# Chunk 2's h by pairs, chunk 1's output in fewer banks, and a new order beside TensorE in chunks 1 and 2

## The chip, the cores and the metric

The kernel runs on one core of a Trainium2 chip. The metric is the device time of one execution in microseconds. Before the change it is 274.47 us, the median of three runs that lie between 274.10 and 274.95.

The engines of the core are TensorE (PE in the profile; PEld is its weight load), VectorE (DVE), ScalarE (ACT), GpSimd (POOL) and SyncE (SP), which here only issues DMAs. Each takes its instructions in the order in which the program lists them; an instruction that waits holds back all that are behind it on the same engine.

## The reference

```python
def _attn_ref(q, k, v) -> np.ndarray:                # q, k, v: (8, 8, 576, 64)
    B, H, S, D = q.shape
    theta = np.pi / 2.0 * np.arange(S) / S
    cos_w, sin_w = np.cos(theta)[None, None, :, None], np.sin(theta)[None, None, :, None]
    def phi(x, c, s):
        r = np.maximum(x, 0.0)
        return np.concatenate([r * c, r * s], axis=-1)
    q_p, k_p = phi(q, cos_w, sin_w), phi(k, cos_w, sin_w)
    kv = np.einsum('bhsf,bhsd->bhfd', k_p, v)
    z = np.sum(k_p, axis=2)
    num = np.einsum('bhsf,bhfd->bhsd', q_p, kv)
    den = np.einsum('bhsf,bhf->bhs', q_p, z)[..., None] + 1e-06
    return num / den

def _moe_ref(x, w_in, w_out, beta):                  # x: (4608, 512), w_in: (512, 2048)
    h = x @ w_in
    g = h * (1.0 / (1.0 + np.exp(-beta * h)))
    return g @ w_out                                 # (4608, 512)
```

The attention's result, with heads side by side, is the `x` of the second function. All is given and returned in float32; the kernel multiplies in bfloat16.

## The kernel before, in words

**Batches and chunks.** The attention is worked by batch, `b` = 0 to 7, with 576 tokens each, the feed-forward part by chunk, `c` = 0 to 8, with 512 tokens each. Nine groups of 64 tokens make a batch (`n` = 0 to 8), eight make a chunk, so chunk 2 takes its tokens from batches 1 and 2. While chunk c is multiplied, batch c + 1 is finished and batch c + 2 is prepared.

**A batch.** Three loads on SP bring q, k and v (1152 KB each, L86, `load_raw`) into `raw_q`, `raw_k`, `raw_v`. There is one buffer of each, so the load of the next batch waits for the last reader of this one. `q_relu` writes `qb` (L200 on ACT, L201 on DVE, two halves), `k_relu` writes `rk`, `v_scale` writes `vb`, nine instructions with the cosine and nine with the sine (L226 on ACT, L228 on DVE). A DMA transposes `qb` to `qt` (`q_turn_dma`, L268, "the turn of q"), and `tan_mul` (L232), on GpSimd in `q_tan` or on DVE, makes `qs` of it. `kv_mm` (L285, 72 small matmuls) and a copy give `kv`. `num_all` (L308), three parts of three token groups, multiplies `qt` and `qs` with it; `x_div` (denominator, reciprocal, product: L320, L324, L331) divides a part, and a DMA transposes it into `xt`, the chunk's input (`x_turn_dma`, L379).

**h of a chunk.** In chunks 0 to 2 it is `h_group` (L425): for each of 16 column blocks `jt` of `w_in` four matmuls of 512 columns (L398) into a PSUM bank, and then a Silu on ACT (L406) into `g`. From jt 4 on the bank is the one of jt - 4. In chunks 3 to 8 it is `h_pair` (eight pairs of blocks): seven products of two matmuls of 256 columns each (L522), with sums of the weights (`w_sum`) and of `xt` (`x_sum`, L466, four on DVE) as operands, and with copies and adds on ACT and DVE between them (`fast_ops`: "c" L491 on ACT copies the first product, "d" or "D" L495 copies the fifth, "e" and "f" L498 add on DVE), then two Silus (L432). Product 3 of a pair needs its add "e", product 4 its add "f".

**Output of a chunk.** Sixteen sums of `g` (`g_sum`, L418, four kinds by four slices, on DVE) and seven products of eight matmuls of 256 columns for each of two halves of the rows. Chunk 1 does this in `o_fast` (L579), with three banks for each half, chunks 2 to 8 in `o_pair` (L637). The rows go out by DMAs of GpSimd's queue (L548).

**Order.** The program is recorded instruction by instruction, without a scheduler. In chunk 0, in chunk 1 and in chunk 2's h the order is that of the Python statements (the loop at `for slot in range(16)`, the `ops` lines behind it, and `h_first`); elsewhere it is the string `ORDERS[c]`, one word for each step, read by `chunk`. Words that the prediction uses: `h13` is product 3 of pair 1, `h1e` that pair's add, `ox1`, `oy1` products of the output, `s12` the g sum of kind 1 and slice 2, `t1` the x sum of kind 1, `N0` and `x0` a part of num and its division, `K0` and `K1` kv, `q1` a relu of q on DVE, `w3` and `v3` scalings of v on DVE and ACT, `g0` a `q_tan`, `TQ` the turn of q, `Lq` a load.

What surrounds the change: before it SP holds, in chunk 1, the turn of batch 2's q, the loads of q, k and v of batch 3, the transposes of x's parts, the turn of batch 3's q, one more transpose of x, and the loads of q and k of batch 4. The relu of batch 3's q is on ACT behind h, that of batch 4's on DVE behind the scalings of batch 3 in chunk 2.

Of the kernel before, what the change touches and what calls it, by code (L numbers as in the profile page):

```python
# [22 lines left out]
def kernel(  # L23
# [234 lines left out]
    def qs_of(b):  # L258
        return wx["q"] if b > 3 and b % 2 == 0 else qs_first
# [311 lines left out]

    def o_fast(c, pr, banks):

        b_ps, e_ps, a_ps = (ps[:, k_, 0:HM] for k_ in banks)
        tok = slice(pr * P, (pr + 1) * P)

        def prod(dst, left, right, start, stop):
            for i in range(JT // 2):
                nc.tensor.matmul(dst, lhsT=left(i), rhs=right[:, i], start=start and i == 0,  # L579
                                 stop=stop and i == JT // 2 - 1, skip_group_check=True)  # L580

        def g_part(r, hf):
            def at(i):
                jt = 2 * i + r
                return gs[c, jt // 4][:, jt % 4, hf * (TCH // 2) + pr * P : hf * (TCH // 2) + (pr + 1) * P]
            return at

        def s_part(t):
            return lambda i: t[:, i, tok]

        o1 = osb_pool.tile([P, DM], FP32, name="o_sb", tag="o_sb")
        o2 = osb_pool.tile([P, DM], FP32, name="o_sb", tag="o_sb")
        p1 = part.tile([P, HM], FP32, name="p1", tag="p1")
        p5 = part.tile([P, HM], FP32, name="p5", tag="p5")
        u = part.tile([P, HM], FP32, name="u", tag="u")

        def c4():
            nc.scalar.copy(o2[:, 0:HM], b_ps)

        def stored(key, op):  # L600
            def do():
                op()
                waits[key[0]].discard(key[1:])
                if not waits[key[0]]:
                    store(c, pr + (2 if key[0] == "2" else 0), o2 if key[0] == "2" else o1)
            return do

        waits = {"1": {"a2", "a3"}, "2": {"a7", "c4"}}
        add = dict(op=ALU.add)
        return {  # L610
            "1": lambda: prod(b_ps, g_part(0, 0), B11, True, False),
            "5": lambda: prod(e_ps, s_part(S[1]), T1, True, False),
            "6": lambda: prod(b_ps, s_part(S[2]), T2, False, False),
            "2": lambda: prod(a_ps, g_part(1, 0), B21, True, True),
            "7": lambda: prod(b_ps, s_part(S[3]), T3, False, False),
            "3": lambda: prod(e_ps, s_part(S[4]), B22, False, True),
            "4": lambda: prod(b_ps, g_part(1, 1), T4, False, True),
            "c1": lambda: nc.scalar.copy(p1, b_ps),
            "c5": lambda: nc.scalar.copy(p5, e_ps),
            "cu": lambda: nc.scalar.copy(u, b_ps),  # L620
            "c4": stored("2c4", c4),
            "a2": stored("1a2", lambda: nc.vector.tensor_tensor(o1[:, 0:HM], a_ps, p1, **add)),
            "a3": stored("1a3", lambda: nc.vector.tensor_tensor(o1[:, HM:DM], e_ps, u, **add)),
            "a7": stored("2a7", lambda: nc.vector.tensor_tensor(o2[:, HM:DM], b_ps, p5, **add)),
        }
# [312 lines left out]
    t_sum(4, 4, 8)  # L938
    for jt in range(4):
        h_mm(1, jt, (0, 1))  # L940
    for slot in range(16):
        if slot < 4:
            h_mm(1, slot, (2, 3))
            h_act(1, slot)
        else:
            h_group(1, slot)
        if slot == 0:
            att_q(2)
            for jp in range(2):
                tan_mul(nc.gpsimd, qs_of(2)[:, jp, 0:1], qts[0][:, jp, 0:1], 0, 1)  # L950
            for tt, o_sb in kept:
                store(0, tt, o_sb)
            v_half(2, 0)
        if 2 <= slot < 6:
            v_half(2, 1, slot + 3, slot + 4, "act")
        if slot == 4:
            k_all(2)
            v_half(2, 1, 0, 5)
            t_sum(3, 0, 8)
        elif slot == 10:  # L960
            num_rest()
            kv_all(2, eng="act")
            x_rest()
            for jp in range(2):
                tan_mul(nc.vector, qs_of(2)[:, jp, 1:], qts[0][:, jp, 1:], 1, NQ)
    def one_sums(kind):
        for i0 in range(0, JT // 2, 2):
            got = g_sum(1, i0, i0 + 2, kind)
        return got

    def ops(of, names):
        for n in names.split():
            of[n]()

    x, y = o_fast(1, 0, (2, 5, 4)), o_fast(1, 1, (3, 7, 6))
    ops(x, "1 c1")
    one_sums(1)
    ops(y, "1 c1")
    q_relu(3, 0, "act")
    q_relu(3, 1, "act")  # L980
    for t, bank in enumerate((4, 6, 0)):
        num_all(2, t, bank)
    one_sums(2)
    x_part(2, 0, 4)
    ops(x, "6 cu")
    ops(y, "6 cu")
    one_sums(3)
    ops(x, "2 5 c5")
    x_part(2, 1, 6)
    q_turn_dma(3)  # L990
    ops(x, "7")
    got = one_sums(4)
    ops(x, "a2 a7")
    ops(y, "7 2")
    x_part(2, 2, 0)
    load_raw(4, "q")
    q_tan(3, 0, got)
    q_tan(3, 1)
    ops(y, "a2 5 c5")
    ops(x, "3 a3 4 c4")  # L1000
    ops(y, "a7 3 a3 4 c4")
    v_half(3, 0)

    ORDERS = {
        2: (
            "ox16 N12 N00 oy17 x0 oxc4 oyc5 ox5 ox6 oxd k2 k0 k3 k1 v5 x1 N20 oxe oy6 v4 v1 v3 oy5 Lk x2 oyD "
            "oye v0 ox7 q1 q0 w2 w8 ox3 ox2 oy3 w1 w3 oy7 w7 oy2 v7 w5 w6 oyf w4 oxf oy4 v8 ox4 oyX v6 oyB w0 "
            "t1 t3 t2 v2 oxA t4 Lv Lq oxB"),
        3: (
            "h012 TQ h213 K00 h2c5 h0c7 K1 h22 kT h05 h25 h06 h26 h0d h02 h2d h110 h15 h311 h1c4 h0e h35 "  # L1010
            "h2e h07 h0f h27 h03 h1d h3d h2f h3c6 h23 h0A h2A h12 h04 h36 h24 h16 h517 "
# [46 lines left out]

    def chunk(c, last):
        b = c + 1  # L1060
        pairs = {f"h{i}": h_pair(c, i) for i in range(JT // 2)} if c > 2 else {}
        pairs.update({"ox": o_pair(c, 0), "oy": o_pair(c, 1)})
        parts = {}
        for op in ORDERS[c].split():
# [26 lines left out]
            elif k_ == "q":  # L1091
                last = q_relu(b + 2, n)
            elif k_ == "g":
                q_tan(b, n, last)
            elif op == "TQ":
                q_turn_dma(b + 1)
            elif k_ == "L":
                load_raw(b + (3 if op == "Lq" else 2), op[1])
        return last

    def h_first(c):
        b = c + 1
        for slot in range(16):
            h_group(c, slot)
            if slot == 0:
                k_all(b)
                v_half(b, 1, 0, 4)
            if 1 <= slot < 6:
                v_half(b, 1, slot + 3, slot + 4, "act")
            if slot == 3:  # L1110
                att_q(b + 1)
            if slot == 8:
                kv_all(b)
            if slot in (3, 7, 11):
                g_sums(c, slot // 2 - 1, slot // 2 + 1)
            elif slot in (13, 15):
                g_sums(c, slot // 2, slot // 2 + 1)

    h_first(2)
    held = None  # L1120
    for c in range(2, NTC):
        held = chunk(c, held)
# [30 lines left out]
```

## Time and profile before

| | |
|---|---|
| median of three runs | 274.47 us |
| the profiled execution, device time | 275.38 us |
| its span | 273.6 us |
| granted TensorE clock | 0.999 |
| chunk 1, h and output (from the timeline) | 50.20 to 79.67 us |
| chunk 2, h and output | 79.67 to 110.21 us |
| chunk 3, h and output | 110.21 to 137.69 us |

Times inside the execution are us from the start of the span. A timeline line gives start, length, engine, source line, operation, tiles, operand shapes, count, and in brackets the idle time just before it and what ended it; several like instructions in a row are merged into one line. "SPq" is SP's queue, where the length is the time that an issue holds SP, not the transfer. Time to landing is from the issue's start to the arrival of the last byte.

### The profile page before, as it was taken

The numbers are of one execution on the slowest core, as the hardware profiler recorded it, in microseconds if no ns is written. First come the engines' busy times: TensorE is split into PE (matmuls) and PEld (weight loads), VectorE is DVE, ScalarE is ACT, GpSimd is POOL, SyncE is SP. The second block draws the span as 40 slices with busy tenths as digits, with TensorE's granted clock in tenths as the row PEclk, the third lists the DMA queues.
The fourth block names the chain that finished last, engine by engine and source line by source line (L and its number), as shares of the span: only waits on it lengthen the run. The fifth ranks groups of instructions, "written<-read, shape, count | busy, mean of one in ns | idle before, by whom it ended". The sixth has DMA issues, their size and how long they took to land.

```text
span 273.6 us, 9005 instructions
## 1 busy us (share of the span) xinstructions
PE 265.8 (97%) x3722; PEld 208.9 (76%) x3722; DVE 221.1 (81%) x586; ACT 189.9 (69%) x390; POOL 64.2 (23%) x87
## 2 busy tenths in 40 slices
PE   7989999999999998999999999999999999999994
PEld 7557455555974587888888888888888888888883
DVE  4877999989979987479988997899589768757852
ACT  5678877787439655899479966996696179418920
POOL 1420000125009500930084009400840060000001
PEclk9999999999999999999999999999999999999999
DMA  7999999999999999994489939933600360005005
GB/s 236 364 394 385 390 389 305 301 240 355 259 176 342 180 342 253 287 311 94 126 217 358 120 58 210 342 71 60 182 3 5 59 184 2 2 21 135 0 2 155
DMA packets 51369, 54.14 MB, mean 198 GB/s; under 512 B 31920, under 2 KB 32448, under 8 KB 51328
## 3 DMA queue, kind: packets, MB, share of 16 engines
q1 hardware_dynamic: 48160, 45.69, 61.3%
q0 software_dynamic: 2784, 7.61, 9.7%
q8 instruction: 29, 0.48, 0.7%
q10 hardware_dynamic: 384, 0.27, 0.4%
q14 instruction: 12, 0.10, 0.1%
HBM read 36.71 MB, written 9.44 MB: 169 GB/s over the span
## 4 chain that ended last, share of the span: by engine, by line
PE 72%; DMA 17%; DVE 6%; SPq 2%; ACT 1%; issue 1%
PE ps L637 28%; PE ps L522 27%; DMA raw_v<-in_v_dram 7%; PE ps L398 7%; DMA raw_q<-in_q_dram 5%; DMA raw_k<-in_k_dram 4%; PE ps L579 4%; DVE vb L228 4%; PE ps L308 3%; PE ps L285 3%; SPq L86 1%; DVE rk L201 1%; SPq L839 1%; ACT vb L226 0%; DVE xs L331 0%
## 5 line engine op out<-in xcount | busy, mean ns | idle before, releaser
L432 ACT ACTIVATE g_t<-ps,beta 128x512 bf16<-128x512 f32 x96 | 60.4, 701 | 1.4 <-PE ps L522 1.3
L548 POOL DMA_DIRECT2D out_dram<-o_sb x58 | 31.1, 543 | 123.3 <-ACT o_sb L674 86.7
L637 PEld LDWEIGHTS <-w_stage 128*128 128x128 bf16 x448 | 43.4, 98 | 5.2
L522 PE MATMUL ps<-w_stage,ws 128*128 128x256 bf16 x288 | 46.5, 272 | 0.1
L398 PE MATMUL ps<-xt,win 128*128 128x512 bf16 (+1 forms) x214 | 42.5, 357 | 0.0
L522 PEld LDWEIGHTS <-ws 128*128 128x128 bf16 x384 | 37.3, 98 | 5.3 <-issue 0.5
L498 DVE TENSOR_TENSOR ps<-ps,p 128x256 f32<-128x256 f32 x74 | 30.5, 428 | 9.7 <-PE ps L522 3.1
L406 ACT ACTIVATE g_t<-ps,beta 128x512 bf16<-128x512 f32 x48 | 31.7, 693 | 7.5 <-PE ps L398 7.3
L637 PEld LDWEIGHTS <-g_t 128*128 128x128 bf16 x336 | 32.2, 98 | 5.5 <-issue 0.9
L398 PEld LDWEIGHTS <-win 128*128 128x128 bf16 x214 | 20.7, 98 | 19.4
L522 PE MATMUL ps<-xt,win 128*128 128x256 bf16 x192 | 32.9, 273 | 0.0
L232 POOL TENSOR_TENSOR qs<-qt,tanr 128x1152 bf16<-128x1152 bf16 (+2 forms) x10 | 17.7, 1781 | 64.2 <-DMA qt<-T 32.3
L522 PEld LDWEIGHTS <-win 128*128 128x128 bf16 x288 | 28.0, 98 | 3.4
L637 PE MATMUL ps<-wout,g_t 128*128 128x256 bf16 x224 | 29.0, 273 | 0.0
L226 ACT ACTIVATE vb<-raw_v,sin 128x256 bf16<-128x256 f32 (+1 forms) x58 | 26.3, 511 | 3.6 <-DMA raw_v<-in_v_dram 3.6
L418 DVE TENSOR_TENSOR w_stage<-g_t 128x512 bf16<-128x512 bf16 (+1 forms) x66 | 25.9, 419 | 3.0 <-ACT g_t L432 1.5
L491 ACT COPY ps<-ps 128x256 f32<-128x256 f32 x62 | 22.5, 382 | 7.8 <-PE ps L637 4.2
L637 PE MATMUL ps<-T,w_stage 128*128 128x256 bf16 x224 | 26.6, 273 | 0.0
L637 PE MATMUL ps<-wout,w_stage 128*128 128x256 bf16 x224 | 26.4, 273 | 0.0
L331 DVE TENSOR_TENSOR xs<-ps,rden 128x768 bf16<-128x768 f32 (+4 forms) x26 | 24.3, 942 | 1.9 <-DMA xt<-xs 1.0
L498 DVE TENSOR_TENSOR ps<-ps,u 128x256 f32<-128x256 f32 x36 | 15.3, 427 | 6.8 <-PE ps L522 5.1
L674 ACT COPY o_sb<-ps 128x512 f32<-128x512 f32 x11 | 6.3, 587 | 20.1 <-PE ps L637 20.1
(115 smaller groups left out, 409.1 us busy)
## 6 DMA issues: line engine op xcount, KB each, us to landing
raw_v<-in_v_dram SPq DMA_DIRECT2D x7, 1152.0 KB, 10.0
raw_k<-in_k_dram SPq DMA_DIRECT2D x7, 1152.0 KB, 9.9
raw_q<-in_q_dram SPq DMA_DIRECT2D x7, 1152.0 KB, 6.5
out_dram<-o_sb POOLq DMA_DIRECT2D x58, 128.0 KB, 5.1
w_stage<-in_moe_w_in_dram SPq DMA_DIRECT2D x6, 512.0 KB, 8.4
w_stage<-in_moe_w_out_dram SPq DMA_DIRECT2D x2, 1024.0 KB, 10.0
w_stage<-in_moe_w_out_dram SPq DMA_DIRECT2D x4, 512.0 KB, 13.3
out_dram<-o_sb SPq DMA_DIRECT2D x10, 128.0 KB, 2.3
```

Of the source, the lines that this page charges most:

```text
L226: got = nc.scalar.activation(o, a, AF.Copy, scale=t[:, n : n + 1])
L232: return eng.tensor_tensor(dst.rearrange("q n (g p) -> q n g p", g=2), src.rearrange("q n (g p) -> q n g p", g=2), tanr[:, n0:n1].unsqueez ...
L331: nc.vector.tensor_tensor(o.rearrange("q j n s d -> q j (n s) d"), nv[:, :, a:z, :, 0:D].rearrange("q j n s d -> q j (n s) d"), rden[:, :, ...
L398: nc.tensor.matmul(ps[:, h_bank(c, jt), i * 64 : (i + w) * 64], lhsT=win[jt // 4][:, mi, (jt % 4) * P : (jt % 4 + 1) * P], rhs=xt[:, i : i ...
L406: return nc.scalar.activation(gs[c, jt // 4][:, jt % 4], ps[:, h_bank(c, jt)], AF.Silu, scale=beta[:, jt : jt + 1])
L418: return nc.vector.tensor_tensor(o, l, r, op=op)
L432: return nc.scalar.activation(gs[c, jt // 4][:, jt % 4], bank, AF.Silu, scale=beta[:, jt : jt + 1])
L491: return nc.scalar.copy(at("a", 0), at("b", 0))
L498: nc.vector.tensor_tensor(dst, at("b", 0), st["p5"], op=ALU.add)
L522: nc.tensor.matmul(dst, lhsT=l[:, g], rhs=r[:, :, g * HP : (g + 1) * HP], start=start and g == 0, stop=g == 1, skip_group_check=True)
L548: (eng or own).dma_start(out=out_v[bb, n][:, m0:m1], in_=o_sb[hf * HP : (hf + 1) * HP, m0:m1])
L637: nc.tensor.matmul(dst, lhsT=l(i), rhs=r[:, i], start=start and i == 0, stop=i == order[-1], skip_group_check=True)
```

## The change

Chunk 2's h is made by `h_pair` like those of chunks 3 to 8, so that `ORDERS[2]` now begins with it and `h_first` goes. It needs the x sums of chunk 2, which chunk 1's list now makes (t3, t1, t2; t4 at the head of chunk 2).

In `o_fast` two of the three accumulators of a half share a bank, so that the two halves take four banks instead of six: `e` lies behind `a`. Product 5 no longer starts its region; product 2, which starts the bank, precedes it.

All other work of chunks 1 and 2 gets a new order. That of chunk 1 is now a list of steps too, each word a small function. Besides `H0` to `H15` (a group of h), `x1`, `y1` (products of the output), `xc1` (its copies, ACT) and `xa2` (its adds, DVE) the words are: `qa`, `qb` the relus of batch 2's q on DVE, `Qa`, `Qb` those of batch 3's on ACT; `qt`, `Qt` the turns of the two; `ql`, `kl`, `vl` the loads of batch 3, `Ql`, `Kl` and, in chunk 2, `.Vl` those of batch 4; `w`, `u` scalings of batch 2's v on DVE with cosine and sine and `v` with sine on ACT, `W`, `V` those of batch 3; `kk` the relu of batch 2's k, `Ka`, `Kb` of batch 3's on ACT; `T0`, `T1` halves of the sum T3 of weights that was one instruction; `nr`, `xr` the last two token groups of batch 1; `z0`, `z1` tan multiplications on DVE, `g0`, `g1` on GpSimd for batch 3; `X0` to `X2` the divisions; `F` one extra matmul into the upper half of bank 6. In chunk 2 `a1`, `a0` are the relus of batch 4's q on DVE, and a point before a word takes it from chunk 1's steps. The list of chunk 2 holds kv of batch 3 (`K01`, `K1`) near its start.

```diff
     def o_fast(c, pr, banks):
-        b_ps, e_ps, a_ps = (ps[:, k_, 0:HM] for k_ in banks)
+        b_ps, a_ps, e_ps = ps[:, banks[0], 0:HM], ps[:, banks[1], 0:HM], ps[:, banks[1], HM:DM]
...
-            "5": lambda: prod(e_ps, s_part(S[1]), T1, True, False),
+            "5": lambda: prod(e_ps, s_part(S[1]), T1, False, False),
...
-    x, y = o_fast(1, 0, (2, 5, 4)), o_fast(1, 1, (3, 7, 6))
...
+    x, y = o_fast(1, 0, (6, 4)), o_fast(1, 1, (7, 5))
+    def one_sum(kind, i):
+        last_sum[:] = [g_sum(1, 2 * i, 2 * i + 2, kind)]
+    def clear_half():
+        nc.tensor.matmul(ps[:, 6, HM:DM], lhsT=ident, rhs=win[0][:, 0, 0:HM], start=False, stop=True,
+                         skip_group_check=True)
...
+        1: (
+            "T0 qb H0 qa u2 w4 w1 u0 qt gs w8 u3 w0 H1 v7 H2 u1 u4 H3 v6 ql H4 kk w2 v5 w6 H5 w3 H6 w5 v8 H7 H8 "
+            "H9 w7 s11 H10 vl nr kl z1 k0 k1 s10 xr kt z0 Qa s20 H11 H12 H13 H14 s12 H15 x1 T1 y1 N0 xc1 N1 yc1 "
+            "s32 F s13 s33 V5 s40 s21 s22 s23 X0 y6 s30 x6 s42 x2 xcu N2 Qb ycu s31 s41 x5 W2 X1 y2 xc5 s43 V3 "
+            "x7 Ka Qt W1 Kb y5 Ql xa2 x3 Kl X2 yc5 W0 V0 V1 y7 xa7 ya2 t3 t1 xa3 ya7 x4 y3 xc4 g0 t2 g1 y4 V2 W5 "
+            "W6 V4 W3 ya3 V6 W4 yc4 V7 W8 W7"),
         2: (
-            "ox16 N12 N00 oy17 x0 oxc4 oyc5 ox5 ox6 oxd k2 k0 k3 k1 v5 x1 N20 oxe oy6 v4 v1 v3 oy5 Lk x2 oyD "
...
+            "h013 h210 h05 h117 .t4 h0D h15 h2c4 h1c5 h16 h22 .V8 h0c6 K01 K1 h1d kT h06 a1 h12 h1e h25 h0e h26 "
+            "h311 h2d .Vl h2e h13 h1A h07 h0f h35 h3d h23 h17 h02 h3c5 h1f h27 a0 h03 h04 h2A h36 h0A h0B h3e "
...
+            "h52 h7e h67 s11 h73 h72 h6f h6A s21 h77 h5A s31 h54 w4 h7f h64 w5 h7A h44 ox16 h74 h5B w6 N00 h4B "
...
-        pairs = {f"h{i}": h_pair(c, i) for i in range(JT // 2)} if c > 2 else {}
+        pairs = {f"h{i}": h_pair(c, i) for i in range(JT // 2)}
...
-    h_first(2)
+    for op in ORDERS[1].split():
+        step[op]()
```

## The prediction

> **What bounds the kernel now.** I read the page's first block, the busy times by stretch, the timelines of PE, SP, DVE and GpSimd in chunks 1 and 2, and the landing times of single loads.
>
> The page, and the busy times of two stretches (chunk 1's h and chunk 2's h):
>
> ```profile
> PE 265.8 (97%) x3722; PEld 208.9 (76%) x3722; DVE 221.1 (81%) x586; ACT 189.9 (69%) x390; POOL 64.2 (23%) x87
> ...
> 50.20:66.00 15.80, 15.62 (x172) 7.65 (x170) 14.28 (x30) 13.20 (x24) 6.49 (x12) 1.00 1.09 310
> 79.60:95.40 15.80, 15.68 (x139) 7.49 (x137) 15.66 (x33) 11.91 (x21) 10.57 (x10) 1.00 0.95 235
> ```
>
> The columns are length, then busy time of PE, PEld, DVE, ACT, POOL, then clock, DMA share, GB/s. TensorE is full; in chunk 2's h DVE is full as well (15.66 of 15.8), and the DMA engines are near full. What TensorE saves counts only if nobody is late for it. PE's timeline there:
>
> ```profile
> 79.67 7.93 PE L398 MATMUL ps<-xt,win 128*128 128x512 bf16 x36
> 87.53 1.92 PE L285 MATMUL ps<-vb,rk 64*64 64x130 bf16 x72
> ...
> 108.47 1.91 PE L637 MATMUL ps<-T,g_t 128*128 128x256 bf16 x16 [0.75 <-DVE o_sb L498]
> 110.21 0.60 PE L522 MATMUL ps<-xt,win 128*128 128x256 bf16 x4
> 110.74 1.22 PE L285 MATMUL ps<-vb,rk 64*64 64x130 bf16 x72
> ```
>
> Chunk 2 runs from 79.67 to 110.21, 30.54 us. Chunk 3, whose h is already by pairs, has the TensorE work that chunk 2 gets; it runs to 137.69 in 27.48. The same 72 kv products take 1.92 in chunk 2 and 1.22 in chunk 3: the first is stretched by waits.
>
> The SP queue (in order, one instruction at a time), and two loads of raw_q alone with their time to landing:
>
> ```profile
> 54.25 3.59 SPq L268 DMA_TRANSPOSE qt<-qb  x1
> 57.94 0.53 SPq L86 DMA_DIRECT2D raw_q<-in_q_dram  x1
> ...
> 75.16 3.46 SPq L268 DMA_TRANSPOSE qt<-qb  x1
> 80.01 0.90 SPq L86 DMA_DIRECT2D raw_q<-in_q_dram  x1
> ...
> L86 SPq DMA_DIRECT2D raw_q<-in_q_dram x1: 528/528/528, 57.9 to 57.9; - x1
> DMA to landing us min/median/max: 6.3/6.3/6.3
> ...
> L86 SPq DMA_DIRECT2D raw_q<-in_q_dram x1: 899/899/899, 80.0 to 80.0; - x1
> DMA to landing us min/median/max: 5.8/5.8/5.8
> ```
>
> A turn of q holds SP for 3.5 us before the next load can be issued, and a block of q needs some 6 us more. Before, nobody hurried: q of batch 3, landed at 64.2, is used by ACT at 68.19; q of batch 4, landed at 85.8, by DVE at 88.28. DVE beside GpSimd:
>
> ```profile
> 81.70 1.35 DVE L201 TENSOR_SCALAR rk<-raw_k 128x2304 bf16<-128x2304 f32 x1
> 82.97 5.39 DVE L228 TENSOR_SCALAR vb<-raw_v,sin 128x256 bf16<-128x256 f32 x4
> ...
> 81.78 5.90 POOL L232 TENSOR_TENSOR qs<-qt,tanr 128x1152 bf16<-128x1152 bf16 x2 [16.57 <-DVE vb L228]
> ```
>
> Four scalings that take 0.27 each elsewhere take 5.39 while GpSimd multiplies: each of the first two ends only with one of GpSimd's multiplications. The adds of a pair (L498), which read PSUM, keep their 0.43 beside GpSimd at 114.5.
>
> **The change part by part.** *TensorE's work.* Chunk 2's 64 products of 512 columns (7.93 less one latency of 0.38, over 35: 0.216 each, 13.8 us) become 112 of 256 (0.109 each, 12.2): -1.6. If all else were in time chunk 2 would take chunk 3's 27.48: -3.06, which includes the 0.75 wait and 0.70 of stretched kv. Chunk 1's kv can lose its stretch too (on the same timeline 60.07 to 61.65, against 1.22): -0.4, since DVE reaches the last scaling near 60.5. F adds one 256-column product, +0.1. Sum without new waits: -3.35.
>
> *Wait 1: Qa in chunk 1.* On DVE T0 (0.69, half of T3's sum) now stands ahead of the two relus of q, so the turn of batch 2 starts on SP near 54.9 instead of 54.25, ends at 58.5, and the load "ql" behind it is issued at 58.55. At 6.3 it lands at 64.85. Before, the relus of this q stood on ACT behind all of h; now Qa, the first, stands between the copy of kv (done near 62.1) and the Silu of h 11. Qa takes 1.16 (two take 2.22 at 68.19), ends at 66.0, the Silu (0.69) at 66.7. h 15 is written into the bank of h 11 (jt modulo 4), so TensorE must wait for it; with the kv stretch gone it gets there at 65.98 - 0.4 - 0.87 = 64.7. Stall 2.0 us. Behind Qa stand five Silus at 0.605, the last done at 69.15; the g sums s13 to s23 (six at 0.34) follow it until 71.2, and y6 reads them: TensorE, through x1, y1 and two num parts at 70.55, waits 0.7 more. Then 12 products of 0.87 and one num part: chunk 1 ends at 82.2, 2.5 later than before.
>
> *Wait 2: a1 in chunk 2.* X0 is behind s23 on DVE (71.2, and 1.37 for denominator, reciprocal and product), four sums and one scaling follow (1.63), then X1, done at 75.6. SP is in order: X1's turn (1.24, as that of a like part at 78.72), q's turn Qt 3.46, and only then "Ql", the load of q for batch 4, at 80.4. Landing after 5.8 to 6.3: 86.2 to 86.7. DVE's a1, the relu of just this, stands third in DVE's list of chunk 2, ahead of h1e, the add that product h13 needs. GpSimd's two multiplications g0, g1 start when Qt lands (5.6 to 6.5 after its start at 76.9, so 82.5 to 83.4) and end 4.8 later, 87.3 to 88.2. a1 reads and writes SBUF like the scalings above, arrives inside the second, and is done with it: 87.9. h1e adds 0.43: h13 at 88.3. TensorE is there at 82.2 + 12 x 0.218 + 1.2 = 86.0. Stall 2.3 us. Behind h13 lie 27.48 - 3.84 = 23.64 us of products: chunk 2 ends at 111.95, against 110.21: +1.75.
>
> *What it does to the rest.* DVE has about 24 us of chunk 2's work behind a1 (16 adds, 16 g sums, three divisions, nine scalings, two relus, four x sums at the rows' durations) and TensorE 23.6: the 3 us of lead that the list gives DVE is gone. In chunk 4 before, DVE is busy 13.55 of 14.2 us in the output and TensorE has no gap, so a lack of lead costs little; bounds 0 and 1.0 (the order of the 0.75 wait), I take 0.15. Chunk 3 on has the same lists; its DVE starts its first add 3.3 us after TensorE, which takes up the lag: 0.
>
> *Edits at no cost.* The multiplications by tan on DVE (z1, z0) come ahead of wait 1's sums and are done near 64.5; N0, which reads them, is due at 67.4 at the earliest. Four banks instead of six for chunk 1's output: x2 waits for X0 to have read bank 4, done at 72.6, and is due at 73.0; without that 0.4 of cover X0 would be the wait. The stores of chunk 1 move behind on GpSimd's queue, nobody waits. v ahead of k on SP (k now issued near 61 instead of 59.22): ACT's Ka would wait to about 74.6; y3 needs the copy behind it only at 80. X2 behind the transposes that still read xs: in before it waits until 76.04, now xa7 stands behind it, due for x4 at 79.5, done by 78.5.
>
> Sum: -3.35 + 2.0 + 0.7 + 2.3 + 0.15 = +1.8. The profiled execution takes 275.38 (span 273.6 and 1.78 around it), 0.9 above the median of the runs, 274.47; the difference goes onto the median: 276.3.
>
> One rule is weighed beside this. The Trainium skill, page "DMA: Bandwidth & Descriptors", section "Queues, rings and completion order", says that each DMA engine takes a queue's descriptors in ring order; by that, issuing k and v later does not speed up q ahead of them, and 6.3 stays. If they shared, q would land as in the quieter 5.8 row, and the sum would be about 0.5 less, 275.8. No row here separates the two.
>
> **The rivals.** *Loads in time, faster.* If a block of q landed within about 4.3 us of its issue (62.9 for wait 1) and in time for a1 at about 81.8 for wait 2, nothing stalls: 274.47 - 3.35 = 271.1. For it: chunks 3 on run such lists without gaps. Against it: no load of a whole raw block lands in under 5.7 here, and SP's turn ahead of it has its 3.5 us in every row. 9%. With wait 1 paid and only a1 free: 274.47 - 3.35 + 2.7 = 273.8; this decides where Ql lands by 84.5. 9%.
>
> *GpSimd does not hold a1.* If a1 falls between g0 and g1, or Qt lands early, a1 is done 0.75 after landing, 87.1, h13 starts at 87.4: +0.85 + 0.15, 275.4; with both landings at 5.8, 274.8. 22%.
>
> The Trainium skill, page "SBUF — State Buffer", section "SBUF: two separate sides", has the port as a lock that the first to start holds for its whole instruction; the trace agrees (5.39 for four).
>
> *GpSimd also holds chunk 2's first kv.* W8 and W7, the last scalings, come at about 82.4; if Qt lands before that, W7 waits for g0 (84.8), t4 for g1 (87.2), a1 comes to 88 and kv, whose copy ACT must take before h311, shifts the silus too; with DVE's lack of lead at its upper end: +1.8 + 1.5, 277.8. 14%.
>
> **How the numbers follow.** Likeliest, both waits and the lock, 46%: 276.3, its own range 275.3 to 277.2 (0.3 for each landing, 0 to 1.0 for the lead). The range 273.7 to 278.0 leaves out the faster case, some of the 273.8 one and a tail above. A measurement here can tell about 0.3%, 0.82 us, so the bounds are 273.65 and 275.29. Faster: the first rival and a third of the second case, 0.12. Same: the rest of that, and two thirds of the case without the lock, 0.21. Slower: 0.67.
>
> **What would show it.** In the changed profile: ACT idle before an L200 of qb with "DMA raw_q" as its end at about 62 to 65; PE idle or stretched before the last L398 of chunk 1; DVE idle before L201 of qb near 84 to 86, then an L201 longer than 0.75 beside a POOL L232; PE idle in the first third of chunk 2's h, ended by DVE L498; no 0.75 wait at chunk 2's end; L398 with 64 fewer and L522 with 112 more. Chunk 3's h should start near 112. Wrong it would be if SP issued Ql before 77, or if q(3) landed before 63.

## The result, and the profile after

The changed kernel takes 281.31 us (median of four runs, 280.44 to 282.39) against 274.49 before: ratio 1.025, 95% interval 1.021 to 1.029. It is slower by 6.8 us. The forecast was slower too, but by 1.8 us, and 281.31 lies outside its range of 273.7 to 278.0. The profiled execution took 282.39 us, its span is 280.6. In the experiments further down only ratios are compared, since before itself has medians from 274.2 to 275.7 there. Executions more than 1.5% above the fastest of the same kernel are left out of the ratios, and where the profiled one was such (e7, e8, e10, e12) no profile is shown.

The page's first block, and its line of the granted clock in 40 slices:

```profile
PE 266.5 (95%) x3768; PEld 213.9 (76%) x3771; DVE 222.5 (79%) x601; ACT 197.3 (70%) x409; POOL 63.1 (22%) x87
...
PEclk9999999999998899998999999999999999999999
```

TensorE was 97% busy before and is 95% busy now, and the 8s in the line of the clock are new. Busy times by stretch say where: chunks 1 to 3 before, chunks 1 to 3 after, then two pairs of neighbouring stretches of 3.4 us after (columns: stretch, length, busy time and count of PE, PEld, DVE, ACT, POOL, then granted clock, DMA share, GB/s).

```profile
50.20:79.67 29.47, 29.29 (x427) 19.82 (x425) 25.31 (x60) 18.51 (x34) 6.49 (x12) 1.00 1.15 290
79.67:110.21 30.54, 29.67 (x395) 19.55 (x392) 27.55 (x65) 20.03 (x39) 10.89 (x11) 1.00 1.02 268
110.21:137.69 27.48, 27.48 (x443) 24.18 (x441) 21.76 (x62) 22.47 (x52) 8.54 (x11) 1.00 0.80 207
...
49.67:81.29 31.62, 30.30 (x428) 19.81 (x426) 28.12 (x70) 22.96 (x43) 8.85 (x16) 1.00 1.07 275
81.29:113.95 32.66, 29.68 (x443) 24.90 (x440) 25.79 (x69) 23.80 (x52) 7.83 (x9) 0.95 0.79 218
113.95:145.30 31.35, 29.24 (x443) 24.73 (x440) 22.04 (x63) 22.04 (x49) 8.18 (x10) 0.95 0.76 218
...
86.25:89.64 3.39, 1.18 (x10) 0.95 (x10) 2.83 (x5) 0.76 (x2) 3.39 (x5) 1.00 1.10 387
89.67:93.05 3.38, 3.38 (x18) 2.43 (x16) 1.86 (x4) 2.89 (x6) 0.05 (x1) 0.50 1.06 355
127.21:130.60 3.39, 1.28 (x54) 0.84 (x50) 1.63 (x6) 1.63 (x4) 0.00 (x0) 1.00 1.39 184
130.63:134.01 3.38, 3.38 (x31) 2.17 (x34) 3.22 (x10) 2.65 (x6) 0.00 (x0) 0.50 0.31 61
```

| us | before | forecast | after |
|---|---|---|---|
| chunk 1 | 29.47 | 31.9 | 31.62 |
| chunk 2 | 30.54 | 29.9 | 32.66 |
| chunk 3 | 27.48 | 27.5 | 31.35 |

The forecast column is before plus the terms of the prediction's sum. Chunk 1 came out close, chunk 2 is 2.7 us longer than forecast and chunk 3 is 3.9 us longer, though nothing in chunk 3's own list was changed. Outside the three, the stretch up to chunk 1 is 0.5 us shorter and the stretch behind chunk 3 is 0.6 shorter. That gives 2.15 + 2.12 + 3.87 - 0.5 - 0.6 = 7.0, the difference of the spans.

Twice TensorE was idle for some 2 us inside a stretch of 3.4 us (3.39 less 1.18, and 3.39 less 1.28), and in the next 3.41 us it was granted half the clock. At half clock 3.41 us do the work of 1.7. The four executions have a mean granted clock of 0.988 or 0.993, two each. One such stretch in some 280 us takes 0.006 off the mean, so by this estimate two executions had one and the other two, the profiled one among them, had two. PE's timeline, the lines with waits and chunk 1's kv:

```profile
59.54 1.91 PE L285 MATMUL ps<-vb,rk 64*64 64x130 bf16 x72
...
66.10 1.02 PE L398 MATMUL ps<-xt,win 128*128 128x512 bf16 x4 [1.09 <-ACT g_t L406]
...
83.03 0.38 PE L522 MATMUL ps<-w_stage,ws 128*128 128x256 bf16 x2 [0.49 <-ACT ps L491]
...
88.46 0.38 PE L522 MATMUL ps<-xt,ws 128*128 128x256 bf16 x2 [2.49 <-DVE ps L498]
...
90.09 0.64 PE L522 MATMUL ps<-w_stage,ws 128*128 128x256 bf16 x2
...
130.10 1.19 PE L637 MATMUL ps<-wout,g_t 128*128 128x256 bf16 x6 [2.11 <-ACT g_t L432]
```

The first wait is h15's, the second h16's, the third h13's; the last is at the first output product of chunk 3. Two products take 0.64 from first start to last end at 90.09, and 0.38 elsewhere. What stood behind these waits, on ACT:

```profile
64.31 1.16 ACT L200 ACTIVATE qb<-raw_q 128x1152 bf16<-128x1152 f32 x1 [2.17 <-DMA raw_q<-in_q_dram]
65.38 2.98 ACT L406 ACTIVATE g_t<-ps,beta 128x512 bf16<-128x512 f32 x5
...
128.97 0.52 ACT L226 ACTIVATE vb<-raw_v,sin 128x256 bf16<-128x256 f32 x1 [2.59 <-DMA raw_v<-in_v_dram]
129.39 3.55 ACT L432 ACTIVATE g_t<-ps,beta 128x512 bf16<-128x512 f32 x6
```

And on DVE, on GpSimd and in SP's queue at the start of chunk 2, then in SP's queue at the start of chunk 3, after and, in the last three lines, before:

```profile
86.67 1.40 DVE L201 TENSOR_SCALAR qb<-raw_q 128x1152 bf16<-128x1152 f32 x1 [4.10 <-DMA raw_q<-in_q_dram]
87.99 0.75 DVE L498 TENSOR_TENSOR ps<-ps,p 128x256 f32<-128x256 f32 x2
...
82.73 4.72 POOL L232 TENSOR_TENSOR qs<-qt,tanr 128x1152 bf16<-128x1152 bf16 x2 [1.27 <-DMA qt<-qb]
...
76.20 2.75 SPq L268 DMA_TRANSPOSE qt<-qb  x1
79.04 0.53 SPq L86 DMA_DIRECT2D raw_q<-in_q_dram  x1
...
112.82 0.52 SPq L86 DMA_DIRECT2D raw_k<-in_k_dram  x1
113.89 0.38 SPq L86 DMA_DIRECT2D raw_q<-in_q_dram  x1
114.39 1.23 SPq L86 DMA_DIRECT2D raw_v<-in_v_dram  x1
115.71 13.25 SPq L268 DMA_TRANSPOSE qt<-qb  x1
...
110.36 0.38 SPq L86 DMA_DIRECT2D raw_v<-in_v_dram  x1
110.81 0.53 SPq L86 DMA_DIRECT2D raw_q<-in_q_dram  x1
111.44 11.71 SPq L268 DMA_TRANSPOSE qt<-qb  x1
```

In these three places (Qa, a1 and `v7`) one instruction waits for a load, and what TensorE needs stands behind it: Silus behind Qa, the add h1e behind a1, and in chunk 3 six Silus behind `v7`, the scaling of v for which the load issued at 114.39 landed only near 128.9. The old list of chunk 2 ended with `Lk`, then far behind it `Lv Lq`: k issued at 104.12, v at 110.36, ahead of q, and landed at 117.72. The new list has `Lk Lq Lv` close together, and v is the last of three blocks.

### The profile page after: what moved, and what is told of

Same layout as the page of the kernel before. It is cut to its first block, busy times and chain, and to the rows that moved or that the text cites. A ratio compares the mean times of both kernels' runs of the same rounds, so it can differ in the third digit from the quotient of the medians.

```text
span 280.6 us, 9133 instructions
## 1 busy us (share of the span) xinstructions
PE 266.5 (95%) x3768; PEld 213.9 (76%) x3771; DVE 222.5 (79%) x601; ACT 197.3 (70%) x409; POOL 63.1 (22%) x87
## 4 chain that ended last, share of the span: by engine, by line
PE 76%; DMA 14%; DVE 4%; ACT 2%; SPq 2%; issue 2%; ACTq 0%; DVEq 0%
PE ps L637 31%; PE ps L522 26%; DMA raw_v<-in_v_dram 9%; PE ps L398 7%; DMA raw_q<-in_q_dram 5%; PE ps L557 5%; PE ps L308 3%; PE ps L285 2%; DVE w_stage L418 1%; ACT g_t L406 1%; SPq L268 1%; DVE xs L331 1%; SPq L86 1%; PE ps L368 1%; DVE rden L324 0%
## 5 line engine op out<-in xcount | busy, mean ns | idle before, releaser
L522 PE MATMUL ps<-w_stage,ws 128*128 128x256 bf16 x336 | 55.4, 275 | 0.5 <-ACT ps L491 0.5
L522 PEld LDWEIGHTS <-ws 128*128 128x128 bf16 x448 | 44.0, 99 | 9.8 <-issue 3.3
L498 DVE TENSOR_TENSOR ps<-ps,p 128x256 f32<-128x256 f32 x85 | 35.2, 429 | 17.2 <-PE ps L522 8.5
L522 PE MATMUL ps<-xt,win 128*128 128x256 bf16 x224 | 38.8, 275 | 0.0
L491 ACT COPY ps<-ps 128x256 f32<-128x256 f32 x70 | 25.6, 382 | 8.9 <-PE ps L637 4.1
L226 ACT ACTIVATE vb<-raw_v,sin 128x256 bf16<-128x256 f32 (+1 forms) x62 | 28.0, 500 | 3.3 <-DMA raw_v<-in_v_dram 3.2
L418 DVE TENSOR_TENSOR w_stage<-g_t 128x512 bf16<-128x512 bf16 x64 | 26.6, 433 | 3.9 <-ACT g_t L406 1.9
L398 PE MATMUL ps<-xt,win 128*128 128x512 bf16 (+1 forms) x150 | 28.5, 348 | 1.1 <-ACT g_t L406 1.1
L398 PEld LDWEIGHTS <-win 128*128 128x128 bf16 x150 | 14.5, 98 | 13.5 <-issue 1.4
L522 PE MATMUL ps<-xt,ws 128*128 128x256 bf16 x112 | 21.0, 275 | 2.5 <-DVE ps L498 2.5
L228 DVE TENSOR_SCALAR vb<-raw_v,cos 128x256 bf16<-128x256 f32 x63 | 19.8, 351 | 2.1 <-DMA raw_v<-in_v_dram 2.1
```

What stands on the lines that cost most here:

```text
L226: got = nc.scalar.activation(o, a, AF.Copy, scale=t[:, n : n + 1])
L228: got = nc.vector.tensor_scalar(o, a, scalar1=t[:, n : n + 1], scalar2=None, op0=ALU.mult)
L398: nc.tensor.matmul(ps[:, h_bank(c, jt), i * 64 : (i + w) * 64], lhsT=win[jt // 4][:, mi, (jt % 4) * P : (jt % 4 + 1) * P], rhs=xt[:, i : i ...
L418: return nc.vector.tensor_tensor(o, l, r, op=op)
L491: return nc.scalar.copy(at("a", 0), at("b", 0))
L498: nc.vector.tensor_tensor(dst, at("b", 0), st["p5"], op=ALU.add)
```

## Experiments

The theory after the first look: the wait of a1 (chunk 2) and the wait of v7 (chunk 3) make the loss, and each is made worse by the half clock that follows it. The rivals: the half clock has another cause, so that the waits alone explain less; or the waits only move when one of them is taken away.

Of the long strings of `ORDERS` the diffs print only the words around each edit. The times of chunks are those of one profiled execution each: chunk 1, whose list is the same in the changed kernel and in e1, e2, e3, e6, e13 and e14, takes 30.49 to 31.88 us there, so a difference of about 1 us in one chunk proves little by itself.

**e1: keep TensorE busy ahead of h13.** 22 products whose result nobody reads.

```diff
-h2e h13
+h2e fill h13
...
+            elif op == "fill":
+                for i in range(22):
+                    nc.tensor.matmul(ps[:, 2, 0:HM], lhsT=ident, rhs=win[0][:, 0, 0:HM], start=True, stop=True,
+                                     skip_group_check=True)
```

> The changed kernel with 22 products of 256 columns into the free bank 2 put on TensorE just ahead of h13; they are extra work, nothing reads them. In the changed profile TensorE waits there 2.49 us and its products take 0.43 instead of 0.22 us per pair for the 3.4 us that follow. Theory (the clock is halved because TensorE stood still): the 22 products fill 2.4 us of the wait, h13 starts at the same 88.5 us, no half clock follows, time falls by half of 3.4, 1.7 us, to about 279.6. Rival (the slow products have another cause, waits inside the queue or the SBUF traffic of that stretch): the products after h13 stay at 0.43, time unchanged at 281.3 or up to 0.3 more.

Measured: ratio 1.0224 (1.017 to 1.0278). In the profile h13 starts at 88.72, as late as without the extra products; there is no half clock behind it, and chunk 2 takes 1.5 us less, 31.15 against 32.66. The half clock in chunk 3 stays. In the ratio to before the gain is only 0.3%, half of what was expected.

```profile
81.49:112.64 31.15, 30.52 (x465) 26.18 (x463) 25.56 (x69) 23.51 (x52) 7.92 (x9) 1.00 0.80 228
112.64:144.49 31.85, 29.27 (x442) 24.79 (x440) 22.00 (x63) 22.05 (x49) 8.19 (x10) 0.95 0.82 215
```

**e2: a1 later,** directly ahead of a0, some twenty steps behind h1e.

```diff
-h06 a1 h12 h1e
+h06 h12 h1e
...
-h27 a0 h03
+h27 a1 a0 h03
```

> The changed kernel with a1, the relu of batch 4's q, moved on DVE from ahead of h1e to just ahead of a0. Theory (h1e is late only because a1 in front of it waits for a load): the 2.49 us wait ahead of h13 and the 1.7 us of half clock behind it go, chunk 2's h is 4.2 us shorter, of which up to 1 us comes back where a1 now stands because the load lands near 86.7; time 277.1 to 278.3. Rival (DVE has too much work in chunk 2's h for the pairs, whatever the order): the adds behind the new place are late instead, the wait moves to h03 or h04, time 280.5 to 281.5.

Measured: ratio 1.017 (1.0123 to 1.0217). Chunk 2 takes 29.52, 3.1 us less than with a1 ahead of h1e, without half clock; the wait of 2.49 is gone, two of 0.49 and 0.44 stay. Chunk 3 keeps its 31.3. So what a1 costs in chunk 2 is about 3.1 us (wait and clock together; the ratio, 0.8% better, says 2.2 us), and the load of v costs the same whether chunk 2 is late or not.

**e3: v ahead of q** at the end of chunk 2's list.

```diff
-Lq oy3 ox4 Lv oyA
+Lv Lq oy3 ox4 oyA
```

> The changed kernel with the last two loads of chunk 2 exchanged on SP: v of batch 5 ahead of q of batch 6. In the changed profile v is issued third, lands at 128.9, and ACT waits 2.59 us for it in chunk 3's h with Silus behind. Theory: v lands 4 to 6 us sooner, before ACT comes to it at 126.4; the 2.11 us wait of TensorE in chunk 3 and its 1.7 us of half clock go: time 277.5 to 278.0. Rival (chunk 3 is late because chunk 2's lag is carried on by DVE and ACT): ACT's wait goes but TensorE still waits for the Silus, time above 280.

Measured: ratio 1.034 (1.0259 to 1.0421), a miss. ACT's wait for v is gone, but TensorE now waits a little further on, and longer, with half clock behind it (PE, then SP's queue):

```profile
132.60 0.26 PE L308 MATMUL ps<-kv,qt 64*64 64x65 bf16 x1 [3.11 <-issue]
...
113.16 1.17 SPq L86 DMA_DIRECT2D raw_q<-in_q_dram  x1
114.42 13.58 SPq L268 DMA_TRANSPOSE qt<-qb  x1
```

The trace names no releaser for this wait. The turn of q, which landed at 132.32, is not it: it is the turn of batch 5, while the product belongs to num of batch 4, whose block was turned in chunk 2. In e6 and e9 the same product waits too, until 2.7 us after the turn has landed. What comes shortly before the end of the wait in e3, e5, e6 and e9 is a packet of 16 KB in the DMA queue that the trace calls "q8 instruction": in e3 it starts at 130.18 and takes 1.08 us, and TensorE goes on 1.3 us after its end (1.3 to 1.5 in the others). So TensorE probably waits for its own instructions. That is argued from the times; no run tests it, and what makes the packet late is not shown.

**e4: Qa later,** behind H15.

```diff
-z0 Qa s20 H11 H12 H13 H14 s12 H15 x1
+z0 s20 H11 H12 H13 H14 s12 H15 Qa x1
```

> The changed kernel with only Qa, the relu of batch 3's q, moved on ACT from ahead of h 11's Silu to behind h 15's. Theory (TensorE's 1.09 us wait ahead of h 15 comes from Qa's load, and all behind it, the turn of q and the load for a1 too, follows 1.2 us earlier): chunk 1 30.3 to 30.6 us instead of 31.6, the wait ahead of h13 stays near 2.5 us, time 279.8 to 280.5. Rival (wait 2 is tied to the loads, not to chunk 1): h13 stays at 88.5 us, the wait ahead of it grows to 3.6, time 281.3.

Measured: ratio 1.0224 (1.0186 to 1.0262). Chunk 1 takes 29.63, 2.0 us less, and h13, at 86.91, still waits 2.43 us. The profiled execution keeps the gain: its span is 278.0 against 280.6, and chunk 3 takes 30.62, since the half clock does not come there although TensorE waits 2.2 us for the Silus as before. In the ratio only 0.3% is seen: two of the four executions have a granted clock of 0.986 and 0.988, two stretches of half clock by the estimate above, the other two 0.993. So wait 1 is real and costs up to 2.0 us in its chunk; its share of the end result is smaller and less sure.

**e5: the three together.** e2, e3 and e4 in one.

> The changed kernel with three instructions moved: a1 to just ahead of a0 on DVE, v of batch 5 ahead of q of batch 6 on SP, and Qa, the relu of batch 3's q on ACT, from ahead of h 11's Silu to behind h 15's. Theory (the change's gain on TensorE is there and was given back by four instructions that wait for loads): about 4 less from a1, 3.8 less from v, 1.1 to 1.8 less from Qa: 271.5 to 273.0, below the kernel before (274.5), and chunk 2 close to the 27.5 us of chunk 3. Rival (too much work beside TensorE): above 275, with chunk 2 over 29 us.

Measured: ratio 1.0164 (1.0085 to 1.0243). Chunks 1 and 2 take 30.02 and 30.12, but chunk 3 takes 32.66, with the wait that e3 showed (3.08) and half clock behind it. Putting v first is not enough for chunk 3.

**e6: only chunk 3's transfers in another order:** k, v, the turn of q, and the next q only behind the turn.

```diff
-Lq oy3 ox4 Lv oyA
+Lv oy3 ox4 oyA
...
-h012 TQ h213
+h012 TQ Lr h213
```

(`Lr` is the load of q as a step of the next chunk's list.)

> The changed kernel with only SP's order at the border of chunks 2 and 3 altered: k, v of batch 5, the turn of its q, and only then the load of q for batch 6. With v alone put first, ACT's wait went but the third part of num then waited 3.1 us for the turn, which landed behind four loads' worth of traffic. Theory (chunk 3's stall is the queue of loads and turn issued together at its start; v and the turn are the two that it needs): chunk 3 27.5 to 28.3 us instead of 31.35, no half clock in it, time 277.3 to 278.3. Rival (the traffic of that stretch as a whole is too much, whatever the order): another wait of 2 us or more in chunk 3, time above 280.

Measured: ratio 1.011 (1.0072 to 1.0148). The stretch of chunk 3, SP's queue, and PE's only wait in chunk 3:

```profile
112.03:140.42 28.39, 27.54 (x442) 24.14 (x440) 21.93 (x63) 21.84 (x49) 8.19 (x10) 1.00 0.87 240
```

```profile
111.96 0.37 SPq L86 DMA_DIRECT2D raw_v<-in_v_dram  x1
112.45 11.63 SPq L268 DMA_TRANSPOSE qt<-qb  x1
124.13 0.58 SPq L86 DMA_DIRECT2D raw_q<-in_q_dram  x1
...
129.62 0.21 PE L308 MATMUL ps<-kv,qt 64*64 64x65 bf16 x1 [0.85 <-issue]
```

Three us of chunk 3's 3.9 come back with two moved loads. The wait of 0.85 is at the product at which e3 waited 3.11; here the packet of instructions starts 15.2 us after the chunk's start, in e3 17.4. The ratio in 274.47 us is 277.5, inside the predicted range: the order of the transfers at this border is the larger half of the miss. Not all of it is chunk 3's: chunk 2 takes 31.20 in this profile and has no half clock, though h13 waits 2.6 us as before.

**e7: e6 with Qa and a1 late.**

> The changed kernel with Qa late, a1 late, v of batch 5 ahead, and q of batch 6 behind the turn. Theory: chunk 1 30.0, chunk 2 29.5 to 30.1, chunk 3 27.5 to 28.3, no half clock before the end, time 273.5 to 275.0, the kernel before within 0.4%. Rival (too much work beside TensorE in chunks 1 and 2): above 277.

Measured: ratio 1.0027 (0.9996 to 1.0059), as before. The three steps taken one at a time gave about 1.4% (e6), 0.8% (e2) and 0.3% (e4), together 2.5%, and at once 2.2%. So the loss of the change is in these three places.

**e8: e7 with the relus of k and the load of k earlier** in chunk 2's output.

```diff
-x0 oyc5 s22
+x0 oyc5 k1 k0 s22
...
-ox5 oyd oy6
+ox5 oyd k2 k3 Lk oy6
...
-oy4 t1 k1 ox7 k0 k2 oxf v8 ox3 k3 v2 oxA w8 q0 Lk w7
+oy4 t1 ox7 oxf v8 ox3 v2 oxA w8 q0 w7
```

> As the run with Qa, a1, v and the turn moved, and ACT's four relus of batch 4's k moved ahead in chunk 2's output, two behind the copy oyc5 and two behind oyd, with the load of k for batch 5 behind them, so that this load is out of the way about 7 us before chunk 3 starts, as it was in the kernel before (issued at 104.1, chunk 3 at 110.2). Theory: the turn of batch 5 lands 2 to 3 us sooner after chunk 3's start, no wait left in chunk 3 (27.5 us), time 273.0 to 274.5. Rival: ACT's relus ahead hold back the copies that oye and oxe add, TensorE waits in chunk 2's output, chunk 2 longer by 1 us or more.

Measured: ratio 1.0158 (1.0129 to 1.0188). A miss; k earlier costs more elsewhere than it brings, and at which instruction stays open.

**e9: e7 with smaller moves,** V7 into chunk 2, a0 behind h3f, and the scalings w4, w5, w6, w0 behind s13.

```diff
-yc4 V7 W8
+yc4 W8
...
-h22 .V8
+h22 .V7 .V8
...
-h27 a1 a0 h03
+h27 a1 h03
...
-h32 h3f h513
+h32 h3f a0 h513
...
-s32 s13 oy5
+s32 s13 w4 w5 w6 w0 oy5
```

> The run with Qa, a1, v and the turn moved (median of its undisturbed runs equal to the kernel before within 0.6%), with the three waits that its chunk 2 still shows taken out by order alone: ACT's V7 behind the copies of pairs 1 and 2 (0.49 us), a0 four adds behind a1 (0.5 us), the four scalings of batch 4 that wait for v behind the g sums instead of ahead of the add h7f (0.7 us). Theory (what is left in chunk 2 is position, not work): chunk 2 about 28.7 us, time 273.0 to 274.2, 0.3 to 0.7% below the kernel before. Rival (DVE's 24 us of work for 27.5 us of TensorE are the bound): new waits of the same sum, chunk 2 30 us, time as the kernel before or above.

Measured: ratio 1.0003 (0.9968 to 1.0038). It equals the kernel before and does not beat it. Its span is 273.1 at clock 1.00; the stretches of chunks 2 and 3, then PE's longest wait in chunk 2:

```profile
79.75:109.40 29.65, 28.61 (x442) 23.89 (x440) 25.60 (x71) 23.67 (x52) 8.89 (x10) 1.00 0.89 241
109.40:137.84 28.44, 27.54 (x443) 24.11 (x440) 21.83 (x63) 21.84 (x49) 8.19 (x10) 1.00 0.88 240
```

```profile
81.49 0.38 PE L522 MATMUL ps<-w_stage,ws 128*128 128x256 bf16 x2 [0.49 <-ACT ps L491]
```

With every large wait gone chunk 2 is 0.9 us shorter than before, not 3.06, and chunk 3 is 1.0 longer than before, 0.9 of it the wait at the product of e3 and e6. From start to start, its 112 products of h take 13.8 us here and 12.4 in chunk 3 before, its 112 of the output 13.0 and 12.3: short waits for adds, sums and copies, each of 0.1 to 0.5 us.

**e10: the turn of q ahead of the load of v** (in e9; `TR` issues it in chunk 2).

```diff
-Lk w7 t2 v6 Lv
+Lk TR w7 t2 v6 Lv
...
-h012 TQ Lr
+h012 Lr
```

> As the smoothed run, with the turn of batch 5's q issued in chunk 2 ahead of the load of v for batch 5 (order on SP: k, turn, v, and q of batch 6 in chunk 3). Theory (in chunk 3 the third part of num waits for the turn because loads stand ahead of it): the wait ahead of num in chunk 3 (0.85 us with the turn behind v) goes, v lands 3.5 us later but still ahead of ACT: chunk 3 27.5 us, time 0.8 less than the smoothed run. Rival (v is the tighter of the two): ACT waits for v, Silus late, chunk 3 29 us or more, time above the smoothed run's.

Measured: ratio 1.0201 (1.0139 to 1.0263). A miss; where e10 waits is not shown.

**e11: GpSimd's g0 and g1 behind a0,** so that nothing of GpSimd runs beside a1 (the last edit makes g0 wait for the relu). a1 stays where the change put it.

```diff
-xc4 g0 t2 g1 y4
+xc4 t2 y4
...
-a0 h03
+a0 .g0 .g1 h03
...
-                q_relu(b + 1, n)
+                last_sum[:] = [q_relu(b + 1, n)]
```

> The changed kernel with GpSimd's two multiplications g0, g1 behind a0 instead of beside a1; a1 stays ahead of h1e. In the changed profile a1 starts when its load lands and takes 1.40 us, 0.65 longer than alone. Theory (GpSimd's instruction holds a1): a1 takes 0.75, h13 starts 0.65 sooner after the landing, the wait ahead of it is 1.8 instead of 2.5 us; the half clock behind it may or may not come, as it depends on where the 3.41 us windows of the clock lie; time 278.5 to 280.7. Rival (a1's length is its own, its source just landed): 1.4 us again, no gain.

Measured: ratio 1.0283 (1.0224 to 1.0341), a miss. a1 takes 0.76 instead of 1.40, but its block lands no earlier, so h13 gains only 0.4 us (88.07 against 88.46). GpSimd's multiplications then run beside DVE's g sums, two of which take 1.26 and 2.27 where one of the changed kernel, alone at 62.21, takes 0.41, and a new wait of 1.74 us follows, with the half clock now behind it (DVE, then PE):

```profile
86.92 0.76 DVE L201 TENSOR_SCALAR qb<-raw_q 128x1152 bf16<-128x1152 f32 x1 [4.53 <-DMA raw_q<-in_q_dram]
92.21 1.26 DVE L418 TENSOR_TENSOR w_stage<-g_t 128x512 bf16<-128x512 bf16 x1
93.72 2.27 DVE L418 TENSOR_TENSOR w_stage<-g_t 128x512 bf16<-128x512 bf16 x1
...
88.07 0.38 PE L522 MATMUL ps<-xt,ws 128*128 128x256 bf16 x2 [2.28 <-DVE ps L498]
96.92 0.38 PE L522 MATMUL ps<-w_stage,ws 128*128 128x256 bf16 x2 [1.74 <-DVE ps L498]
```

**e12 to e14: is it idleness that brings the half clock?** Extra products in chunk 3 ahead of `N03`, in the bank that N03 is about to use: e12 has 18 of them and the 22 of e1, e13 the 18 alone, e14 has 9 and the 22. The step `fill3` is that of e1 with bank 3 and these counts.

```diff
-h43 h4A N03
+h43 h4A fill3 N03
```

> As the run with 22 extra products ahead of product h13, and 18 more (256 columns into bank 3, 0.109 us each, 2.0 us, extra work whose result nobody reads) in chunk 3 ahead of N03, where TensorE otherwise stands 2.1 to 2.6 us ahead of the first output product. No wait is made shorter. Theory (an idle stretch of TensorE of 2 us or more has the next 3.41 us granted at half clock, 1.7 us lost): no stretch of half clock remains in chunks 1 to 3, granted clock 0.999 or 1.0, chunk 2 about 31.1 us as with the first extra products, chunk 3 31.85 - 1.7 = 30.2 us, the time about 1.7 us below that run's and 3.2 below the changed kernel's: ratio to before 1.013 to 1.017. Rival (the half clock is given for something else, such as the load on the DMA engines or TensorE's sum of work, and only falls together with the waits): the half clock stays in chunk 3, which takes 31.5 us or more, and the ratio stays at 1.02 or above.

> Only the 18 extra products in chunk 3 ahead of N03 (extra work whose result nobody reads), none in chunk 2. Theory (an idle stretch of about 2 us brings a stretch of half clock): the half clock ahead of h13 stays (granted clock of the execution 0.993 or 0.994), that in chunk 3 goes; chunk 3 takes 31.35 - 1.7 = 29.6 us; ratio to before 1.018 to 1.021. Rival A (not the idleness of TensorE but the load brings it): two stretches stay, clock 0.988, ratio 1.025. Rival B (the extra products cost elsewhere what they save, since they hold N03 back by 2 us, and with it the division that DVE makes of it): the half clock goes but a new wait of 0.5 us or more stands in chunk 3's output, ended by DVE; ratio 1.022 to 1.025.

> Both places, but only 9 extra products in chunk 3 (1.0 us, half the dose), so that N03 is held back by 1.0 us instead of 2.0 and 1.1 to 1.6 us of the idle time ahead of the first output product stay. Theory with the bound from the windows so far (1.70 us idle in a window of 3.41 us was never followed by half clock, 1.90 always): no half clock in chunks 2 and 3, granted clock 0.997 to 1.0, ratio 1.012 to 1.017. Rival A: clock 0.993 or less, ratio at 1.02 or above. Rival B (extra products ahead of N03 cost by their delay): better than with 18 of them, by up to 1 us.

Measured: e12 ratio 1.0184 (1.014 to 1.0228), clock 0.997 to 0.999 in six of seven executions; e13 1.0284 (1.0254 to 1.0313), clock 0.993 to 0.994; e14 1.0214 (1.0175 to 1.0254), clock 1.000 in all four runs. The stretches of chunks 2 and 3 of e13, then of chunk 3 of e14:

```profile
81.29:114.02 32.73, 29.62 (x443) 24.80 (x441) 25.28 (x69) 23.72 (x52) 7.83 (x9) 0.95 0.83 218
114.02:144.69 30.67, 30.01 (x460) 25.89 (x458) 22.27 (x64) 21.95 (x49) 8.19 (x10) 1.00 0.79 222
```

```profile
113.60:143.85 30.25, 28.87 (x452) 24.95 (x449) 21.97 (x63) 21.85 (x49) 8.20 (x10) 1.00 0.85 222
```

That idleness brings the half clock is shown: e1 has the extra products in chunk 2 and keeps the half clock in chunk 3, e13 has them in chunk 3 and keeps it in chunk 2, and with both, in e14, there is none. The price is smaller than was expected of these runs. Chunk 3 gains 0.7 (e13) and 1.1 us (e14), not 1.7: from start to start the extra products and what is left of the wait take 2.65 and 2.56 us, where the wait alone took 2.28, and num takes 0.5 and 0.2 longer than in the changed kernel (2.05 and 1.74 against 1.54); why it does is not shown. e14 also shows how loose the load of a1 is: issued at 78.4 it landed near 88.5, where a1 starts, 10 us later, against 7.6 in the changed kernel's profile, and chunk 2 takes 33.27 without any half clock. e13's ratio is no better than the changed kernel's, so in the median nothing was gained by it.

How much idleness it takes can be read off the profiles, roughly. The clock changes lie on a grid of 3.41 us. Where TensorE was idle for 1.90 us or more within one such window (nine windows, in the changed kernel, e1 to e5, e11 and e13), the next had half clock; where it was idle for 1.86 us or less (e3, e6, e11, e14), it had not. One window does not fit: in e12's profile, which is not printed here, half clock followed 1.80 us. So the idle time alone, as the profile has it, does not draw a sharp line. The pair that lies closest, window and next window of e4 and of e3:

```profile
82.98:86.37 3.39, 1.50 (x34) 1.13 (x23) 1.55 (x1) 0.96 (x2) 3.39 (x3) 1.00 1.02 397
86.40:89.78 3.38, 2.87 (x14) 2.06 (x14) 2.09 (x7) 1.94 (x4) 1.76 (x4) 0.50 1.13 328
```

```profile
84.75:88.14 3.39, 1.55 (x37) 1.18 (x27) 0.49 (x1) 0.96 (x2) 3.39 (x3) 1.00 1.02 406
88.16:91.55 3.39, 2.73 (x25) 2.34 (x24) 2.96 (x8) 2.32 (x6) 1.92 (x4) 1.00 1.13 299
```

Both kernels have the same wait ahead of h13, 2.43 us in e4 and 2.52 in e3. In e3 it falls across the border of two windows, and chunk 2 takes 31.13 us against 32.32. The same wait can cost over a us more or less by where it falls.

## Why the prediction was wrong

Its direction and its two waits held. The steps that failed are the 0 for chunk 3, the missing term for the clock and, smaller, the gain of 0.4 in chunk 1's kv.

*TensorE's work, -3.35.* The smaller products are there (TensorE's 0.75 us wait at the end of chunk 2 is gone too), but the terms around them did not all come. Chunk 1's kv did not lose its stretch: from its first start to the next product it takes 1.84 us, 1.58 before, so the -0.4 became +0.26. DVE was done with the scalings at 60.57, as predicted, but TensorE came to them at 59.54 and not at 60.07. The 0.15 for DVE's lost lead fits the changed kernel: nearly nothing is left over in the sum below, and chunk 2's 112 products of the output take 12.3 us from start to start, as in chunk 3 before. But there TensorE is late itself. With the large waits gone, "chunk 2 would take chunk 3's 27.48" does not hold: in e9 it takes 29.65, with some 2 us of short waits (0.65 of them at h16), more than the bound of 1.0 that the prediction gave to a lack of lead.

*Wait 1, +2.0 and +0.7.* The mechanism is as predicted: q(3) took 6.4 us to land (predicted 6.3), Qa took 1.16, and counted from the start of the chunk (49.67; 50.20 in the prediction) h15 was released at 16.4 us, predicted 16.5. The wait was 1.09 instead of 2.0 because TensorE came to h15 at 15.3 us, not at 14.5: most of the difference went into the stretched kv. The output's waits behind it, y6's 0.7 in the prediction, come to 0.4 (112 products of 12.76 us from start to start, 12.33 before). The wait was too short and the kv too long, and the errors cancel: chunk 1 is 2.15 us longer, 2.4 were forecast. That is partly luck, since the same list of chunk 1 takes up to 1.1 us less in other profiles. e4, which moves Qa alone, takes 2.0 of it back.

*Wait 2, +2.3.* Predicted: h13 at 88.3 after a stall of 2.3. Measured: 88.46 after 2.49. a1 was held by GpSimd as predicted, 1.40 us instead of the 0.75 to 0.76 it takes alone, but it did not end with GpSimd's second multiplication: that ends at 87.45, a1 at 88.07, 0.62 later (0.62 in e1, e4 and e13 too). Part of the agreement is luck: the turn held SP for 2.75 us, not 3.46, so that SP issued the load at 79.04, not 80.4, and the load took 7.6 us (to a1's start), not 5.8 to 6.3. Neither 6.3, which the prediction kept by the ring order of the Trainium skill's page "DMA: Bandwidth & Descriptors", section "Queues, rings and completion order", nor 5.8 would have given the 7.6, or the 10 of e14; what slowed this load was not tested.

*A small wait not foreseen.* h16 waits 0.49 us for ACT's copy (L491), and does so in every variant.

*"Chunk 3 on has the same lists ...: 0".* This is the step that failed most. Chunk 3's instructions are the same, but its transfers are issued by the end of chunk 2's list, which the change rewrote. The prediction followed SP's queue up to chunk 2's first third and stopped there. (It also says that a turn holds SP for 3.5 us "in every row"; at this border, before, it is 11.71.) The border shows it by itself: the new list has k, q, v where the old one had k, v, q. The cost was 3.9 us, and e6 takes 3.0 of it back with two moved loads.

*No term for the clock.* Both long waits were followed by 3.41 us at half clock. In chunk 2 that is worth 1.5 us (e1, and e3 and e6 by chance), in chunk 3 0.7 to 1.1 net. The profile before had no such stretch in these chunks. The Trainium skill, page "TensorE: Matmul & The Clock Gate", section "What's actually happening", gives half clock after an idle window of about 3.4 us. The trace agrees on the length of the window and on the half; here 1.9 us of idle time within a window was enough, less than the Trainium skill asks.

*The rivals.* "GpSimd does not hold a1" gave that hold a price of 0.9 us (276.3 less 275.4); e11 measures 0.4 at h13, and shows that the hold only moves to other instructions. "GpSimd also holds chunk 2's first kv" did not come: that kv takes 1.22 us, as it does unstretched. "Loads in time, faster" is nearly what e9 makes, and it ends at 1.0003, not at the 271.1 us of that rival: chunk 2 keeps its short waits and chunk 3 is 1.0 us longer than before. None of the rivals had chunk 3 or the clock in it.

*Summed.* Chunk 2's 2.7 us beyond the forecast are, from start to start, 0.65 for h16, 0.35 for the longer wait at h13 and 1.7 for the clock. That leaves short waits of about the 0.15 that the forecast already has for the lost lead. Chunk 3's 3.9 are 2.3 for the wait and 1.6 for the half clock behind it. Of the 1.6 only 0.7 to 1.1 came back where the half clock alone was taken away.

## What to carry to other kernels

When a list of work is rewritten, follow every queue to the first use of everything that it issues, into the stage after the change: a stage whose own list is untouched can still lose most, because its transfers are issued by the stage before. A wait of about 2 us on TensorE is to be priced with the clock that follows it (up to 1.5 us more here). And smaller products count only as far as the engines that feed them have lead: of the 3.06 us hoped for in chunk 2, 0.9 came with every large wait removed.

## What the runs showed of the hardware

- TensorE went to half clock for one window of 3.41 us after each of nine windows in which it was idle for 1.90 us or more, and not after windows with 1.86 (e3), 1.70 (e6) or less; once, in e12, it did so after 1.80 us. What exactly is counted is not shown.
- SP is held by a turn of q for 2.75 us at 76.20, but for 13.25 us when the turn is issued behind three loads (landing 17.6 us after its issue). What stands behind it on SP waits that long: in e6 the load issued next starts at 124.13, after a turn of 11.63 us from 112.45.
- A load of 1152 KB took from 5.6 to 14.6 us from issue to landing in the changed kernel's profile: 5.6 for k at 140.27, 6.4 for q at 57.83, 14.6 for v at 114.39. What makes the difference was not separated.
- GpSimd's multiplications hold up what DVE runs on SBUF beside them: a1 takes 1.40 beside GpSimd and 0.76 without it, a g sum 2.27 and 0.41.
- TensorE stood for 0.85 to 3.1 us at one product of chunk 3 (e3, e5, e6, e9) without a releaser in the trace, and went on 1.3 to 1.5 us after the end of a 16 KB packet in the DMA queue "q8 instruction". That it waited for instructions is likely, not tested.
